# Scaling and shifting the float64 weights' upper words on GpSimd instead of VectorE, in a linear-attention and feed-forward kernel

## The chip, the cores and the metric

The kernel runs on one core of one Trainium2 chip, in one launch. The metric is the device time of one execution in microseconds (us): before the change the median of three runs is 903.01 us (902.7 to 903.02). The engines are called by the names of the profile: PE is TensorE (PEld its weight loads), DVE is VectorE, ACT is ScalarE, POOL is GpSimd, SP is SyncE, which here only starts DMAs.

## The reference

```python
# q, k, v: (8, 8, 576, 64) float32; g_norm: (64,); w_in: (512, 2048), w_out: (2048, 512), both float64
kv  = np.einsum('bhsd,bhse->bhde', k, v)
out = np.einsum('bhsd,bhde->bhse', q, kv)
rms = np.sqrt(np.mean(out * out, axis=-1, keepdims=True) + 1e-06)
x = (out / rms * g_norm).transpose(0, 2, 1, 3).reshape(4608, 512)
h  = x @ w_in
sp = np.maximum(h, 0.0) + np.log1p(np.exp(-np.abs(h)))     # softplus
return ((h * erf(sp)) @ w_out).astype(np.float32)
```

The two weight matrices are float64 in memory. The kernel reads each number as two 32-bit words, an upper and a lower one, and makes float32 of them itself.

## The kernel before, in words

**Tiling.** The 4608 tokens are worked through in nine groups of 512 (T = 0 to 8): the first 512 tokens of each of the eight batches, and a ninth group of the eight remainders of 64. For one group the attention gives x, transposed, as four blocks of 128 features by 512 tokens. The hidden width of 2048 is cut into 16 units of 128 (f = 0 to 15). For unit f, PE multiplies x with a block of w_in (tile `h_ps`, line 1021), ACT copies the result and takes its softplus and erf, DVE multiplies the two (`gates`, line 902, tile `h_sb`), and PE multiplies that with a block of w_out into four accumulators (`o_ps`, `project`, line 655), five units later (`LAG`). From T = 1 on, numbers are split into a rounded upper part and a remainder, so that PE can use its faster float32 form (line 599, tiles `n_ps` and `m_ps`); the split weights are written to device memory once and loaded again for later groups.

**The stage that the change touches** is T = 0, after the start-up, from about 32 to 116 us. There the float64 weights are fetched and converted, in 18 steps listed in `w_order`: four steps of one unit of w_in (512 words per partition), then 14 steps of two units (1024 words per partition), alternately of w_in and w_out. I call them by matrix and first unit: in0, in1, in2, in3, in4, out0, in6, out2, in8, out4, in10, out6, in12, out8, in14, out10, out12, out14. Each step has three parts, each of which goes through the list with an index of its own:

- `load_w` (lines 233 and 238) starts the DMA on SP's queue into `w_raw`. That tile has four buffers.
- `w_split` makes `w_m` from the lower words on ACT (line 260). For the first five steps, which fall in the start-up, it also makes `w_e` on ACT, the upper words times 2**-112 as floats (line 259). `w_e` and `w_m` have two buffers each.
- `w_join` finishes the step on DVE: for the later 13 steps (flag `late_`) it makes that product itself (line 270); it shifts `w_e` left by three bits (line 273), puts the sign bit back from the upper words (line 276), and adds `w_m` (line 281) into `w_in_sb` or `w_out_sb`, from which PE reads.

One call of `weights()` runs `w_split`, then `w_join`, then `load_w`, in this order. In the loop over the units the splits are one step ahead of the joins: a call splits step i+1 and joins step i. The order of each engine's instructions is the order in which the program emits them (`manual_schedule`); each engine works through its own list in that order and waits where an operand is not ready.

**Other DVE work of this stage**, placed between the joins, belongs to the attention of group 1, which runs beside: `keep_tail` (lines 433, 360, 361), `halve` (lines 447, 448, tiles `sq_hi` and `sq_lo`), `norm` (lines 483, 486, 495), and the transposition of q (line 336). `sq_hi` and `sq_lo` are read by the PE products of `mean` (lines 463 and 464), and the transposed q by those of `visit` (line 411).

POOL clears two tiles, builds the identity for the transposes, starts six small DMAs and scales one column (line 221), all in the first 11 us, and has nothing after that.

Of the kernel before, what the change touches and what calls it, by code (L numbers as in the profile page):

```python
# [39 lines left out]
FP32 = mybir.dt.float32  # L40
FP32R = mybir.dt.float32r
I32 = mybir.dt.int32
U32 = mybir.dt.uint32
AF = mybir.ActivationFunctionType
ALU = mybir.AluOpType
# [23 lines left out]
def kernel(  # L69
# [10 lines left out]
    nc = tc.nc  # L80
    P = 128
# [3 lines left out]
    G = J * P  # L85
# [7 lines left out]
    const = ctx.enter_context(tc.tile_pool(name="const", bufs=1))  # L93
# [117 lines left out]
    for p in range(NP):  # L211
        nc.gpsimd.dma_start(
            out=q_last[p % 2 * R : p % 2 * R + R, p // 2],
            in_=q[0, 2 * p : 2 * p + 2, G:S, :].rearrange("h r d -> r h d"),
        )
    for i in range(2):
        nc.gpsimd.dma_start(
            out=g_col[i * D : i * D + D, :], in_=g_norm.rearrange("(d one) -> d one", one=1)
        )
    gm_col = const.tile([P, 1], FP32, name="gm_col")  # L220
    nc.gpsimd.tensor_scalar(out=gm_col, in0=g_col, scalar1=-0.5, scalar2=None, op0=ALU.mult)
    x_last = const.tile([P, KC, G], FP32, name="x_last")
# [20 lines left out]
    def words(which, f):  # L243

        raw = w_raw[which, f]
        hi, lo = (
            raw.bitcast(kind).rearrange("p (n two) -> p n two", two=2)[:, :, half]
            for kind, half in ((FP32, 1), (U32, 0))
        )
        return hi, lo, raw.rearrange("p (n two) -> p n two", two=2)[:, :, 1]  # L250

    def w_split(which, f, k):


        hi, lo, _ = words(which, f)
        e = early.tile([P, G * k], I32, name="w_e", tag="w_e", bufs=2)
        m = early.tile([P, G * k], I32, name="w_m", tag="w_m", bufs=2)
        if not w_late:
            nc.scalar.activation(e.bitcast(FP32), hi, AF.Copy, scale=2.0**-112)
        nc.scalar.activation(m, lo, AF.Copy, scale=2.0**-29)  # L260
        w_cv[which, f] = e, m, bool(w_late)

    def w_join(which, f, k):


        scaled, _, hi = words(which, f)
        e, m, late_ = w_cv.pop((which, f))
        w_raw.pop((which, f))
        if late_:
            nc.vector.tensor_scalar(  # L270
                out=e.bitcast(FP32), in0=scaled, scalar1=2.0**-112, scalar2=None, op0=ALU.mult
            )
        nc.vector.tensor_scalar(
            out=e, in0=e, scalar1=3, scalar2=None, op0=ALU.logical_shift_left
        )
        nc.vector.scalar_tensor_tensor(  # L276
            out=e, in0=hi, scalar=-(1 << 31), in1=e, op0=ALU.bitwise_and, op1=ALU.bitwise_or
        )
        out_ = (w_in_sb if which == "in" else w_out_sb)[f // 2][:, f % 2 : f % 2 + k]
        out_ = out_.rearrange("p t f -> p (t f)")  # L280
        nc.vector.tensor_tensor(out=out_.bitcast(I32), in0=e, in1=m, op=ALU.add)  # L281
# [10 lines left out]
    def w_next(what):  # L292
        i = w_at[what]
        if i < len(w_order):
            w_at[what] = i + 1
            {"load": load_w, "split": w_split, "join": w_join}[what](*w_order[i][1:])
# [809 lines left out]
    def part(h, half):  # L1106
        return h[:, :, half * 2 * P : half * 2 * P + 2 * P]
# [35 lines left out]
    for m in range(first_batch, batches + 1):  # L1143
# [81 lines left out]
        for j in range(J):  # L1225
# [3 lines left out]
            if b2 == NB - 1:  # L1229
                e = es.pop(j)  # L1230
# [14 lines left out]
            for half in due_halves:  # L1245
                nc.vector.tensor_tensor(  # L1246
                    out=part(h, half), in0=part(h, half), in1=part(s, half), op=ALU.mult
# [38 lines left out]
```

## Time and profile before

| what | value |
|---|---|
| median of three runs | 903.01 us |
| span of the profiled execution (first to last instruction) | 901.3 us |
| PE busy | 893.6 us, 99% of the span |
| DVE busy | 766.7 us, 85% |
| ACT busy | 595.1 us, 66% |
| POOL busy | 4.7 us, 1%, 14 instructions |
| granted PE clock, mean | 0.999 of full speed |

The profile is of one execution, and its span leaves out what lies around the first and the last instruction: the median of the runs is 1.7 us longer. A line of a timeline gives the start in us, the length in us, the engine, the source line, the operation, the tile written and the tiles read, the shape, and how many instructions are merged; in brackets behind it stand the idle time before it and what ended that. A line of a group gives the summed busy time in us, the mean of one instruction in ns, and the idle time before them. Steps of PE's 128x512 float32 products appear as two instructions each.

### The profile page before, as it was taken

What the parts mean: (1) busy time and instruction counts of PE and PEld (TensorE: products, weight loads), DVE (VectorE), ACT (ScalarE), POOL (GpSimd) and SP (SyncE); (2) the same over time, 40 slices, a digit from 0 to 9 for tenths busy, and PEclk for the clock granted to TensorE, in tenths of its full rate; (3) what the DMA queues carried; (4) which work ended last, traced back from release to release, by engine and by line L of the source; (5) the groups of instructions that cost most, each with busy time, mean ns of one, the idle gap of its engine ahead of it and who ended that gap; (6) DMA issues with size and microseconds to landing.
All of it is one profiled execution on the core that took longest, in us unless ns stands there. A gap on an engine that the chain in (4) does not pass through costs nothing.

```text
span 901.3 us, 13468 instructions
## 1 busy us (share of the span) xinstructions
PE 893.6 (99%) x4962; PEld 672.4 (75%) x4962; DVE 766.7 (85%) x1105; ACT 595.1 (66%) x789; POOL 4.7 (1%) x14
## 2 busy tenths in 40 slices
PE   8999999999999999999999999999999999999998
PEld 4444456666788888888888888888888888888887
DVE  5899978899799888888888888888888888886667
ACT  5976687777766666666766666666666666665552
POOL 2000000000000000000000000000000000000000
PEclk9999999999999999999999999999999999999999
DMA  9977418899699987988899979988897787778871
GB/s 285 295 224 226 108 73 319 305 341 355 233 384 355 347 301 258 382 308 297 273 361 336 320 248 335 365 300 292 286 341 273 270 304 309 286 282 323 317 263 51
DMA packets 136929, 259.89 MB, mean 288 GB/s; under 512 B 78816, under 2 KB 87264, under 8 KB 136864
## 3 DMA queue, kind: packets, MB, share of 16 engines
q1 hardware_dynamic: 136128, 258.09, 81.3%
q8 instruction: 39, 0.64, 0.3%
q10 hardware_dynamic: 544, 0.82, 0.3%
q14 instruction: 26, 0.21, 0.1%
q0 software_dynamic: 192, 0.13, 0.0%
HBM read 224.40 MB, written 34.60 MB: 287 GB/s over the span
## 4 chain that ended last, share of the span: by engine, by line
PE 96%; DMA 1%; DVE 1%; ACT 1%; issue 0%; SPq 0%; DVEq 0%
PE n_ps L599 50%; PE m_ps L599 25%; PE o_ps L655 9%; PE h_ps L1021 5%; PE at_ps L425 2%; PE at_ps L411 2%; PE n_ps L918 1%; PE at_ps L463 1%; PE at_ps L464 1%; DMA q_sb<-in_q_dram 1%; DMA w_raw<-in_moe_w_out_dram 1%; PE o_ps L918 0%; DVE w_e L276 0%; PE o_ps L722 0%; DVE w_in_sb L281 0%; PE ms_ps L729 0%
## 5 line engine op out<-in xcount | busy, mean ns | idle before, releaser
L599 PE MATMUL n_ps<-w_out_parts,g_forms 128*128 128x512 f32 (+1 forms) x936 | 230.7, 389 | 0.0
L599 PE MATMUL n_ps<-x_forms,w_in_parts 128*128 128x512 f32 x896 | 223.9, 392 | 0.0
L599 PEld LDWEIGHTS n_ps<-w_out_parts,g_forms 128*128 128x128 f32 x936 | 173.7, 188 | 35.3
L599 PEld LDWEIGHTS n_ps<-x_forms,w_in_parts 128*128 128x128 f32 x896 | 166.6, 188 | 35.3
L574 DVE TENSOR_TENSOR h<-m_ps,h 128x512 f32<-128x512 f32 x116 | 78.2, 687 | 60.3 <-PE m_ps L599 58.1
L599 PE MATMUL m_ps<-w_out_parts,g_forms 128*128 128x512 f32 x464 | 124.0, 389 | 0.0
L599 PE MATMUL m_ps<-x_forms,w_in_parts 128*128 128x512 f32 x448 | 119.7, 389 | 0.0
L1192 ACT ACTIVATE h<-n_ps 128x512 f32<-128x512 f32 x112 | 66.2, 594 | 75.1 <-PE n_ps L599 75.0
L1197 ACT ACTIVATE s<-h 128x512 f32<-128x512 f32 x112 | 68.3, 629 | 70.0 <-DVE h L574 70.0
L599 PEld LDWEIGHTS m_ps<-w_out_parts,g_forms 128*128 128x128 f32 x464 | 87.1, 188 | 18.5
L599 PEld LDWEIGHTS m_ps<-x_forms,w_in_parts 128*128 128x128 f32 x448 | 84.1, 188 | 17.5
L574 DVE TENSOR_TENSOR e<-m_ps,e 128x512 f32<-128x512 f32 x116 | 80.2, 692 | 15.2 <-PE m_ps L599 5.3
L655 PE MATMUL o_ps<-w_out_sb,h_sb 128*128 128x512 f32 x192 | 86.8, 595 | 0.0
L540 DVE SCALAR_TENSOR_TENSOR g_forms<-g_forms 128x1024 fp32r<-128x1024 f32 x58 | 71.1, 1225 | 2.0
L537 DVE TENSOR_TENSOR g_forms<-h,g_forms 128x1024 fp32r<-128x1024 f32 x58 | 70.6, 1217 | 1.2 <-ACT g_forms L534 1.1
L534 ACT ACTIVATE g_forms<-h 128x1024 fp32r<-128x1024 f32 x58 | 58.4, 1049 | 15.5 <-PE m_ps L599 11.1
L569 DVE SCALAR_TENSOR_TENSOR e<-n_ps,e 128x512 f32<-128x512 f32 (+1 forms) x89 | 60.4, 678 | 6.9 <-PE n_ps L599 6.9
L1246 DVE TENSOR_TENSOR h<-h,s 128x1024 f32<-128x1024 f32 x56 | 65.9, 1218 | 0.0
L655 PEld LDWEIGHTS o_ps<-w_out_sb,h_sb 128*128 128x128 f32 x192 | 35.5, 190 | 38.3 <-issue 36.9
L1021 PE MATMUL h_ps<-xT,w_in_sb 128*128 128x512 f32 x128 | 57.9, 596 | 1.1 <-DVE w_in_sb L281 1.1
L115 ACT ACT_TABLE_LOAD x43 | 55.2, 1283 | 0.8
L1220 ACT ACTIVATE s<-s 128x1024 f32<-128x1024 f32 x50 | 50.6, 1053 | 0.3
(148 smaller groups left out, 1018.7 us busy)
## 6 DMA issues: line engine op xcount, KB each, us to landing
w_out_parts<-w_out SPq DMA_DIRECT2D x116, 768.0 KB, 6.8
w_in_parts<-w_in SPq DMA_DIRECT2D x112, 768.0 KB, 6.7
w_in<-w_new SPq DMA_DIRECT2D x16, 768.0 KB, 4.9
k_sb<-in_k_dram SPq DMA_DIRECT2D x32, 288.0 KB, 5.9
v_sb<-in_v_dram SPq DMA_DIRECT2D x31, 288.0 KB, 5.8
w_raw<-in_moe_w_in_dram SPq DMA_DIRECT2D x16, 512.0 KB, 5.9
w_raw<-in_moe_w_out_dram SPq DMA_DIRECT2D x8, 1024.0 KB, 5.1
out_dram<-e SPq DMA_DIRECT2D x32, 256.0 KB, 3.8
```

What stands on the lines that cost most here:

```text
L115: nc.scalar.preload_act_table_set("softplus")
L534: nc.scalar.activation(high, x, AF.Copy, scale=1.0 + 2.0**-13)
L537: nc.vector.tensor_tensor(out=low, in0=x, in1=high.bitcast(FP32), op=ALU.subtract)
L540: nc.vector.scalar_tensor_tensor(out=both, in0=low.bitcast(FP32), scalar=SHIFT, in1=high.bitcast(FP32), op0=ALU.mult, op1=ALU.add,)
L569: nc.vector.scalar_tensor_tensor(out=out_, in0=ps, scalar=scale, in1=out_, op0=ALU.mult, op1=ALU.add)
L574: nc.vector.tensor_tensor(out=out_, in0=ps, in1=out_, op=ALU.add)
L599: nc.tensor.matmul(ps[:, cols], lhsT=weights(form, k), rhs=moving(form, k)[:, cols], start=(form == forms[0] and k == 0), stop=(form == fo ...
L655: nc.tensor.matmul(o_ps[j], lhsT=g[:, j * P : j * P + P], rhs=one(w_out_sb, f), start=(f == 0), stop=last,)
L1021: nc.tensor.matmul(plain[i], lhsT=blocks_of(one(w_in_sb, i % FC))[:, c], rhs=xT[T][:, c, :], start=(c == 0), stop=(c == KC - 1),)
L1192: nc.scalar.activation(h[:, i], n_ps, AF.Copy, scale=SHIFT - 1.0)
L1197: nc.scalar.activation(s[:, i], h[:, i], AF.Softplus)
L1246: nc.vector.tensor_tensor(out=part(h, half), in0=part(h, half), in1=part(s, half), op=ALU.mult)
```

## The change

The product with 2**-112 of the later 13 steps moves from DVE, where `w_join` issued it, to POOL, where `w_split` issues it, one call earlier in the program. The shift by three of these steps becomes a 32-bit integer multiplication by eight on POOL, issued in `w_join`; its second operand is a new column tile `eight`, set once by DVE and read as if it were as wide as the step. The first five steps stay as they were.

```diff
@@ -217,6 +217,8 @@
+    eight = const.tile([P, 1], I32, name="eight")
+    nc.vector.memset(eight, 8)
     gm_col = const.tile([P, 1], FP32, name="gm_col")
@@ -257,6 +259,10 @@  (w_split)
         if not w_late:
             nc.scalar.activation(e.bitcast(FP32), hi, AF.Copy, scale=2.0**-112)
+        else:
+            nc.gpsimd.tensor_scalar(
+                out=e.bitcast(FP32), in0=hi, scalar1=2.0**-112, scalar2=None, op0=ALU.mult
+            )
         nc.scalar.activation(m, lo, AF.Copy, scale=2.0**-29)
@@ -267,12 +273,13 @@  (w_join)
         if late_:
+            nc.gpsimd.tensor_tensor(
+                out=e, in0=e, in1=eight.to_broadcast([P, G * k]), op=ALU.mult
+            )
+        else:
             nc.vector.tensor_scalar(
-                out=e.bitcast(FP32), in0=scaled, scalar1=2.0**-112, scalar2=None, op0=ALU.mult
-            )
-        nc.vector.tensor_scalar(
-            out=e, in0=e, scalar1=3, scalar2=None, op0=ALU.logical_shift_left
-        )
+                out=e, in0=e, scalar1=3, scalar2=None, op0=ALU.logical_shift_left
+            )
         nc.vector.scalar_tensor_tensor(
             out=e, in0=hi, scalar=-(1 << 31), in1=e, op0=ALU.bitwise_and, op1=ALU.bitwise_or
         )
```

## The prediction, made before the changed kernel was run

> **What bounds the kernel now.** I read the page's head first, then busy time by stretches, then the waits and the timelines of the stage that is changed. Head (busy us, share, instructions) and three stretches (start:end, length, busy PE, PEld, DVE, ACT, POOL, clock, DMA share, GB/s):
>
> ```profile
> span 901.3 us, 13468 instructions
> PE 893.6 (99%) x4962; PEld 672.4 (75%) x4962; DVE 766.7 (85%) x1105; ACT 595.1 (66%) x789; POOL 4.7 (1%) x14
> ```
> ```profile
> 50.00:60.00 10.00, 9.62 (x25) 4.41 (x24) 9.66 (x13) 6.53 (x8) 0.00 (x0) 1.00 0.88 277
> 80.00:90.00 10.00, 10.00 (x69) 4.72 (x69) 9.53 (x16) 4.17 (x5) 0.00 (x0) 1.00 0.81 252
> 120.00:901.00 781.00, 777.44 (x4322) 617.32 (x4320) 667.49 (x948) 509.88 (x674) 0.00 (x0) 1.00 0.84 300
> ```
>
> PE is the bound everywhere, and after 120 us it is busy for 777.44 of 781 us: time lost earlier is not made good. DVE is nearly full in the changed stage, yet PE hardly waits for it. PE's only wait there is 0.39 us for in6, and the waits of the whole start and stage for `w_in_sb` are 1.1 us:
>
> ```profile
> 51.15 3.70 PE L1021 MATMUL h_ps<-xT,w_in_sb 128*128 128x512 f32 x8 [0.39 <-DVE w_in_sb L281]
> ...
> 114.63 0.68 PE L463 MATMUL at_ps<-sq_hi,mean_w 128*128 128x256 f32 x1
> ```
> ```profile
> PE h_ps L1021 <- DVE w_in_sb L281: 1.1, 2, 0.7
> ```
>
> So relief of DVE is worth at most some 0.4 us. What counts is whether DVE falls behind, since PE has a margin on it. The end of out0 and the joining of out12 in DVE's timeline, with what stands behind it:
>
> ```profile
> 42.41 1.23 DVE L281 CUSTOM_DVE_ANT_0 w_out_sb<-w_e,w_m 128x2048 uint16<-128x2048 uint16 x1
> ...
> 105.02 0.69 DVE L270 TENSOR_SCALAR w_e<-w_raw 128x1024 f32<-128x1024 f32 x1
> 105.74 0.69 DVE L273 TENSOR_SCALAR w_e<-w_e 128x1024 int32<-128x1024 int32 x1
> 106.47 1.23 DVE L276 SCALAR_TENSOR_TENSOR w_e<-w_raw,w_e 128x1024 int32<-128x1024 int32 x1
> 107.83 1.23 DVE L281 CUSTOM_DVE_ANT_0 w_out_sb<-w_e,w_m 128x2048 uint16<-128x2048 uint16 x1
> 108.97 0.68 DVE L902 TENSOR_TENSOR h_sb<-h_sb,s_sb 128x512 f32<-128x512 f32 x1
> 109.57 0.42 DVE L447 CAST sq_hi<-qT 128x512 fp32r<-128x512 f32 x1
> 110.03 0.69 DVE L448 TENSOR_TENSOR sq_lo<-qT,sq_hi 128x512 fp32r<-128x512 f32 x1
> ```
>
> From the end of out0 (42.41 + 1.23 = 43.64) to that of out12 (107.83 + 1.23 = 109.06) lie 11 steps in 65.42 us, 5.95 us each. `sq_lo` behind out12 ends at 110.72, and PE reads it after 114.63: a margin of 3.9 us. The gate at 104.42 (ends 105.1, wanted by line 655 at 108.06) has 3.0 us, others 3 to 7. The weights have far more from out2 on (out8: 15 us).
>
> **What leaves DVE.** 13 pairs of lines 270 and 273 at 0.72 us each from start to start (105.02, 105.74, 106.47): 13 x 1.45 = 18.8 us. PE waits for none of it but in6, so its worth is 0 to 0.4 us.
>
> **What comes to POOL.** It shows no such instruction, so I bound both by its small ones (mean ns of one before the bar's idle time):
>
> ```profile
> L210 POOL MEMSET bd_kv<- 128x256 f32 x1 | 0.3, 311 | 0.0
> masks.py:199 POOL TENSOR_SCALAR_AFFINE_SELECT ident<-ident 128x128 f32<-128x128 f32 x1 | 0.3, 292 | 0.1
> L221 POOL TENSOR_SCALAR gm_col<-g_col 128x1 f32<-128x1 f32 x1 | 0.2, 218 | 4.9 <-DMA g_col<-in_g_norm_dram 4.9
> masks.py:197 POOL MEMSET ident<- 128x128 f32 x1 | 0.2, 205 | 0.3 <-POOLq L1267 0.3
> ```
>
> The memsets give (311 - 205) / 128 = 0.83 ns a word and 99 ns fixed. One input, 128 words, takes 292 ns. If 218 ns of that is fixed (line 221), a word costs 0.58 ns and the scaling of 1024 words 0.81 us; if only 99 ns is, 1.51 ns and 1.64 us. I take the middle, 1.2 us. The multiplication reads two tensors: at least 0.8 us, as if the second were free; at most twice 1.51 ns a word, 3.2 us; I take two readings, 2 x 1.2 - 0.2 = 2.2 us. The pair is 3.4 us (1.6 to 4.8).
>
> **The new wait.** In POOL's list the scaling of step i+1 stands ahead of the multiplication of step i. The scaling needs the `w_e` buffer that line 281 of step i-1 frees, and line 276 of step i now waits for the multiplication. So the steps form a ring: line 281, POOL's pair, line 276, line 281. Its DVE part is 109.06 - 106.47 = 2.59 us; three handovers at 0.05 (PE started at 51.15 after DVE's end at 51.10) make some 0.2. One turn is 2.59 + 3.4 + 0.2 = 6.19 us, and 11 turns 68.1 against 65.4: DVE is 2.7 us late at out12. Behind the waiting line 276 on DVE are queued line 281, the gates, and group 1's `halve` and `norm`; PE waits for gates and `sq_lo`. The first turn costs nothing: in6's DMAs are issued by 31.7 us and take 5.9 (median), POOL would be through with scaling in6 and multiplying out0 at 37.6 + 3.4 = 41.0, and line 276 ran at 41.05.
>
> **Other DVE work during POOL's pair.** If DVE and POOL can read memory at once, that work lies beside the pair. If not, it lengthens the ring. DVE's instructions with two tensors from SBUF, or at double rate, between the ends of out0 and out12 are nine gates at 0.60 (108.97 to 109.57), three of line 486 at 0.72, and two of `halve` at 1.07 (109.57 to 110.64): 5.4 + 2.2 + 2.1 = 9.7 us. No row shows the engines together: the bounds are 0 and 9.7. The nearest rows are lines 273 and 276: one tensor of 1024 words takes 0.69 us, two take 1.23, so DVE alone has no third stream to spare. I take 9.7 and keep 0 for the range.
>
> [...]
>
> **Edits at nothing.** Setting `eight` is 0.06 us (line 203's length, the same shape) in DVE's 3.8 us of idle time before 6.22. SP's load for step i+4 is issued when line 276 of step i ends, with group 1's q, k and v behind it; four steps are some 24 us and a landing 5 to 8, so a slip of a few us stays hidden; uncovered, it would hold PE at line 411 by its own length. ACT's line 260 waits for `w_m` in the same ring, and copies of `h_ps` stand behind it; ACT idles 1.5, 5.3 and 6.5 us before the copies at 84, 93 and 115, and `h_ps` has two buffers. The new tile may shift others in SBUF; no row prices that, I take 0.
>
> **Sum.** 2.7 + 9.7 = 12.4 us late at out12, less the margin of 3.9: PE loses 8.5 us, in pieces from about 85 us on. The profiled execution becomes 901.3 + 8.5 = 909.8 and the median, 1.7 above its span as before, 911.5. This case alone spans 905 to 919.
>
> **Rivals.**
> *The pair fits (not slower).* Without blocking, 2.7 us late is under 3.9 and PE never waits: 903.0, or 902.6 if in6's wait also goes. It decides as long as blocking plus 11 x (pair - 3.16) stays below 3.9 us. For it: DVE's order leaves 3.4 us beside the weights in each step. Against it: half of that work has two inputs.
> *POOL is slow.* At 4.8 us a pair the ring is 7.59, 11 turns 83.5, 18.1 late; with blocking and the margin 18.1 + 9.7 - 3.9 = 23.9: 927. The point is a pair above 4 us. For it: an integer product of full words, of which POOL shows no row.
> *The relief counts.* If DVE's 18.8 us were on the path it would be faster; PE's busy rows from 60 to 110 us, full in every stretch, speak against it.
>
> **How the numbers follow.** Forecast 0.50, slow POOL 0.22, the pair fits 0.24, faster by something unseen 0.04. About 0.2% (1.8 us) is what a measurement can tell from no change; the fitting pair lies within it, so slower has 0.72. The range goes from 902.4 (the pair fits) to 926, leaving out the end of slow POOL and a real gain, some 0.15.
>
> **What would show it.** Right: POOL's pairs stand back to back in every step, lines 276 wait for POOL, steps are over 6.2 us apart, gates lie late or long, PE waits for `sq_lo` and gates between 85 and 116 us, and DVE's busy time falls by about 18 us. Wrong: a pair below 3 us, gates and POOL overlapping at their old lengths, or PE's loss after 120 us.

## The result, and the profile after

The changed kernel takes 932.71 us (median of four runs, 931.31 to 934.05) against 903.01 us: a ratio of 1.033, with a 95% interval of 1.0317 to 1.0343. The forecast was 911.5 us, range 902.4 to 926. The direction was right, the size was not: 29.7 us were lost where 8.5 were expected, and the time lies beyond the range.

In the changed file the lines behind the new code are seven higher: the scaling is line 263, the multiplication 276, the sign line 283, the addition 288, the gates 909, PE's unit products 1028, the projection 662, the mean 470. The head of the page after, and the busy time by stretches (start:end, length, busy PE, PEld, DVE, ACT, POOL, clock, DMA share, GB/s):

```profile
span 930.6 us, 13490 instructions
PE 907.6 (98%) x4962; PEld 675.9 (73%) x4962; DVE 756.6 (81%) x1080; ACT 595.7 (64%) x789; POOL 69.6 (7%) x40
```
```profile
50.00:60.00 10.00, 7.47 (x20) 3.49 (x19) 3.29 (x4) 6.02 (x8) 7.12 (x4) 1.00 0.55 171
90.00:100.00 10.00, 7.03 (x55) 3.36 (x50) 4.53 (x5) 2.72 (x4) 5.65 (x3) 0.83 0.45 121
150.00:930.00 780.00, 776.35 (x4309) 615.13 (x4307) 663.05 (x943) 505.10 (x668) 0.00 (x0) 1.00 0.87 298
```

PE is no longer full in the stage, and POOL is busy in 7 of 10 us there. DVE is idle for more than half of a stretch in which it was 97% busy. In the second stretch even the granted clock is below 1 (0.83). The waits of the start and the stage (who waited for whom: us in all, times, longest) say for what:

```profile
DVE w_e L283 <- POOL w_e L276: 35.2, 10, 4.7
PE o_ps L662 <- DVE h_sb L909: 6.5, 4, 3.0
PE at_ps L470 <- DVE bd_kv L368: 4.9, 2, 2.9
PE h_ps L1028 <- DVE w_in_sb L288: 3.5, 3, 2.5
```

That is the ring of the prediction: PE for DVE, DVE for POOL. One turn of it on POOL, without and with a gate beside it, then the last ones on DVE and the last wait of PE:

```profile
62.44 2.88 POOL L263 TENSOR_SCALAR w_e<-w_raw 128x1024 f32<-128x1024 f32 x1 [2.71 <-DVE w_out_sb L288]
65.26 1.92 POOL L276 TENSOR_TENSOR w_e<-w_e,eight 128x1024 int32<-128x1024 int32 x1
70.32 3.26 POOL L263 TENSOR_SCALAR w_e<-w_raw 128x1024 f32<-128x1024 f32 x1 [3.13 <-DVE w_in_sb L288]
73.55 1.88 POOL L276 TENSOR_TENSOR w_e<-w_e,eight 128x1024 int32<-128x1024 int32 x1
```
```profile
44.25 1.23 DVE L283 SCALAR_TENSOR_TENSOR w_e<-w_raw,w_e 128x1024 int32<-128x1024 int32 x1 [4.05 <-POOL w_e L276]
45.62 1.22 DVE L288 CUSTOM_DVE_ANT_0 w_out_sb<-w_e,w_m 128x2048 uint16<-128x2048 uint16 x1
...
132.19 1.23 DVE L288 CUSTOM_DVE_ANT_0 w_out_sb<-w_e,w_m 128x2048 uint16<-128x2048 uint16 x1
...
135.85 0.29 DVE L368 TENSOR_TENSOR bd_kv<-at_ps,kv_other 128x128 f32<-128x128 f32 x1
```
```profile
136.29 0.55 PE L470 MATMUL at_ps<-sq_hi,mean_w 128*128 128x256 f32 x1 [2.85 <-DVE bd_kv L368]
...
137.28 6.17 PE L662 MATMUL o_ps<-w_out_sb,h_sb 128*128 128x512 f32 x8
```

The scaling takes 2.85 to 2.88 us where no gate runs beside its start and 3.2 to 3.3 where one does (as in the last two lines on POOL); the multiplication takes 1.9. out0's joining now ends at 46.84 and out12's at 133.42: 11 turns in 86.58 us, 7.87 each, where there were 65.42 us.

The 29.3 us by which the span grew come apart at two marks of PE. The last wait ends at 136.29, where the same product began at 114.63 before: 21.7 us, start-up included. From there to the first product of T = 1 2.7 us more are lost, nearly all in the eight projections at 137.28, which took 3.59 us before and 6.17 now. That product before and after:

```profile
128.82 0.80 PE L599 MATMUL n_ps<-x_high,w_new 128*128 128x512 f32 x1
```
```profile
153.19 0.79 PE L606 MATMUL n_ps<-x_high,w_new 128*128 128x512 f32 x1
```

From that product to the end lie 772.5 us before and 777.4 after: 4.9 us, all of them without a wait.

### The profile page after: what moved, and what is told of

Same layout as the page of the kernel before. It is cut to its first block, busy times and chain, and to the rows that moved or that the text cites. A ratio compares the mean times of both kernels' runs of the same rounds, so it can differ in the third digit from the quotient of the medians.

```text
span 930.6 us, 13490 instructions
## 1 busy us (share of the span) xinstructions
PE 907.6 (98%) x4962; PEld 675.9 (73%) x4962; DVE 756.6 (81%) x1080; ACT 595.7 (64%) x789; POOL 69.6 (7%) x40
## 4 chain that ended last, share of the span: by engine, by line
PE 87%; POOL 6%; issue 3%; DVE 1%; ACT 1%; DMA 1%; SPq 0%; POOLq 0%; DVEq 0%
PE n_ps L606 49%; PE m_ps L606 24%; PE o_ps L662 6%; POOL w_e L263 4%; POOL w_e L276 2%; PE h_ps L1028 2%; PE at_ps L432 2%; PE at_ps L418 2%; PE n_ps L925 1%; PE at_ps L470 1%; DMA q_sb<-in_q_dram 1%; PE at_ps L471 1%; DVE w_e L283 1%; PE o_ps L925 0%; DVE w_out_sb L288 0%
## 5 line engine op out<-in xcount | busy, mean ns | idle before, releaser
L606 PE MATMUL n_ps<-w_out_parts,g_forms 128*128 128x512 f32 (+1 forms) x936 | 230.9, 389 | 0.0
L606 PE MATMUL n_ps<-x_forms,w_in_parts 128*128 128x512 f32 x896 | 226.6, 395 | 0.0
L662 PE MATMUL o_ps<-w_out_sb,h_sb 128*128 128x512 f32 x192 | 94.2, 638 | 6.5 <-DVE h_sb L909 6.5
L662 PEld LDWEIGHTS o_ps<-w_out_sb,h_sb 128*128 128x128 f32 x192 | 38.2, 205 | 50.1 <-issue 41.1
L283 DVE SCALAR_TENSOR_TENSOR w_e<-w_raw,w_e 128x1024 int32<-128x1024 int32 (+1 forms) x18 | 22.5, 1247 | 36.9 <-POOL w_e L276 35.2
```

The costliest lines, as they stand in the source:

```text
L606: nc.tensor.matmul(ps[:, cols], lhsT=weights(form, k), rhs=moving(form, k)[:, cols], start=(form == forms[0] and k == 0), stop=(form == fo ...
L662: nc.tensor.matmul(o_ps[j], lhsT=g[:, j * P : j * P + P], rhs=one(w_out_sb, f), start=(f == 0), stop=last,)
```

## The experiments

Each kernel is compared with the kernel before on the same chip; its median was 903.0 to 903.2 us.

**The new tile's place.** The loss behind the stage had no wait in it, and the loads had become slower; so I looked at the one thing that stays after the stage, the tile `eight` ahead of others in memory. To the kernel before I added only:

```diff
+    eight = const.tile([P, 1], I32, name="eight")
+    nc.vector.memset(eight, 8)
     gm_col = const.tile([P, 1], FP32, name="gm_col")
```

> The kernel before with the column tile eight and its memset added, and nothing on POOL. In the changed kernel the products of T = 1 to 8 take 4.5 us longer without any wait (PE busy 773.15 us from the first product of T = 1 on, against 768.64 before), loads into SBUF land later (w_in_parts 7.7 us against 6.7), and the start-up is 0.5 us longer. Theory place: this comes from where the new tile pushes the tiles behind it, so this kernel takes 903.0 + 5 = 908 us with landings of 7.7 us. Rival: it comes from the later timing of the stage or from the chip's state, and this kernel takes 903.0 within 0.5 us, landings 6.7 us.

It took 907.95 us, ratio 1.0051 (1.0038 to 1.0065). A line of a DMA group gives KB each and us from issue to landing; first the lines of the kernel before:

```profile
w_out_parts<-w_out SPq DMA_DIRECT2D x116, 768.0 KB, 6.8
w_in_parts<-w_in SPq DMA_DIRECT2D x112, 768.0 KB, 6.7
```
```profile
L599 PE MATMUL n_ps<-x_forms,w_in_parts 128*128 128x512 f32 x896 | 223.9, 392 | 0.0
L599 PE MATMUL m_ps<-x_forms,w_in_parts 128*128 128x512 f32 x448 | 119.7, 389 | 0.0
```

With the new tile:

```profile
PE 898.8 (99%) x4962; PEld 673.2 (74%) x4962; DVE 766.6 (85%) x1106; ACT 595.5 (66%) x789; POOL 4.7 (1%) x14
```
```profile
w_out_parts<-w_out SPq DMA_DIRECT2D x116, 768.0 KB, 7.7
w_in_parts<-w_in SPq DMA_DIRECT2D x112, 768.0 KB, 7.8
```
```profile
L601 PE MATMUL n_ps<-x_forms,w_in_parts 128*128 128x512 f32 x896 | 226.6, 395 | 0.0
L601 PE MATMUL m_ps<-x_forms,w_in_parts 128*128 128x512 f32 x448 | 121.2, 392 | 0.0
```

PE is busy 5.2 us longer with the same products. It is mainly the products with w_in's parts that grew (223.9 and 119.7 us before; 4.2 of the 5.2 us), not those with w_out's, whose buffers are laid out from the other end of the memory and did not move (230.9 after 230.7). The loads of w_out's parts landed later all the same, so a later landing alone did not lengthen the products. So a tile of one column cost 4.9 us, and none of it is POOL's.

The other way round, the changed kernel without the unused tile `pad` ahead of `eight`:

```diff
-    const.tile([P, 8], FP32, name="pad")
```

> The changed kernel without the unused tile pad, which stands ahead of eight in the same pool, so that the tiles behind lie where they lay before. Theory place: 932.7 - 5 = 927.7 us, landings of w_in_parts back to 6.7 us, PE busy after the first product of T = 1 back to 768.6 us; the rest of the loss, some 24.7 us, stays. Rival (the tile's place does nothing): 932.7 us.

It took 922.99 us, ratio 1.0229 (1.0203 to 1.0255): 9.7 us less than the changed kernel, though its four runs spread from 921.43 to 928.05. Landings of `w_in_parts` are back at 6.6 us. The gain is larger than the place alone: with the loads earlier, POOL scales in6 at 36.46 rather than 39.51, line 282 for out0 runs at 41.20 rather than 44.25, and only two stretches of half clock are left.

How far may the tiles move? An unused tile of 64, 512 or 2048 bytes a partition in the kernel before, and `eight` with 32 bytes more ahead of w_in's buffers:

```diff
+    const.tile([P, 16], I32, name="eight")     # 512 bytes: [P, 128]; 2048 bytes: [P, 512]
     gm_col = const.tile([P, 1], FP32, name="gm_col")
```

> The kernel before with an unused tile of 64 bytes a partition where the changed kernel has eight (which takes 32 with its rounding, as pad does). Theory line: what costs 4.9 us is that the tiles behind start 32 bytes off a multiple of 64; a shift by 64 costs nothing: 903.1 us, landings 6.7 us. Rival (any shift from the old places costs): 906 to 908 us.

> The kernel before with an unused tile of 512 bytes a partition at the place of eight. Shifts of 32 and 64 bytes cost 4.9 and 4.1 us. If what counts is a start at a multiple of 512 bytes or less, this takes 903 us and w_in_parts land in 6.7 us; if the multiple is larger, or the old places matter for another reason, 906 to 908 us with landings of 7.4 us or more.

> The same with 2048 bytes, the length of one buffer row of 512 words. If what counts is where the tiles start within 2048 bytes, this takes 903 us with landings of 6.7 us; if any move from the old places costs, 906 to 908 us.

64 bytes cost as much as 32, nearly: 907.04 us (ratio 1.0045, 1.003 to 1.006), landings 7.4 us; a shift by 64 is no protection, and that theory fell. 512 bytes cost nothing: 903.06 us (0.9999, 0.999 to 1.0008), landings 6.8; nor do 2048: 902.8 us (1.0, 0.999 to 1.0009). And `eight` with the 32 bytes more:

```diff
+    eight = const.tile([P, 1], I32, name="eight")
+    nc.vector.memset(eight, 8)
...
+    ctx.enter_context(tc.tile_pool(name="shift_w", bufs=1)).tile([P, 8], FP32, name="shift_w")
     w_in_p = ctx.enter_context(tc.tile_pool(name="w_in_p", bufs=BATCH))
```

> The kernel before with eight (908.0 us by the earlier run) and a further 32 bytes ahead of the buffers of the loaded weights of w_in (and what lies behind them), so that these start at multiples of 64 again while the tiles for k, v, q, x and the sums do not. If the weights' loads are what makes PE's products slower, landings go back to 6.7 us and the time to 903.5 to 904.5 us (0.5 us is the start-up's). If it is x and the others, it stays near 908.

This missed both expectations: 910.9 us (1.0088, 1.0073 to 1.0103), landings 8.0, w_in's products 229.1 and 122.7 us. It moves w_in's buffers by 64 bytes in all and x's by 32, and is worse than moving both by 32 or both by 64. Which of the two tiles of a product counts stays open.

Landings took 7.4 to 8.0 us after shifts of 32 and 64 bytes, 6.8 and 6.9 after 512 and 2048. No shift between 64 and 512 bytes was run, so where the loss ends is not shown. Nor is it shown why the loads landed later: those of w_out's parts, which were not moved, did so as well (7.6 to 7.8 us against 6.8). Why PE's products slow down too, no run shows.

**The ring.** First the order of POOL's two instructions, the multiplication of step i ahead of the scaling of step i+1:

```diff
...
         else:
+            times_eight()                      # the multiplication for the step before
             nc.gpsimd.tensor_scalar(
                 out=e.bitcast(FP32), in0=hi, scalar1=2.0**-112, scalar2=None, op0=ALU.mult
             )
+            to_eight.append((e, k))
...
         if late_:
-            nc.gpsimd.tensor_tensor(
-                out=e, in0=e, in1=eight.to_broadcast([P, G * k]), op=ALU.mult
-            )
+            if to_eight and to_eight[0][0] is e:
+                times_eight()
```

> The changed kernel with POOL's two instructions the other way round: the multiplication of step i is issued ahead of the scaling of step i+1, so a joining no longer waits for the next step's scaling. Theory ring: the loss of the stage comes from both instructions (3.2 + 1.9 us) lying between the end of one joining and the start of the next; now two steps share a ring of 2.6 + 5.1 + 0.3 = 8 us, far under 2 x 5.95, PE never waits, and the time is that of place alone, 908 us. Theory lock: DVE's two-input instructions and POOL's cannot run at once; a step needs 2.46 (lines 283 and 288) + 0.9 (gates, halve, norm) + 5.1 (POOL) = 8.5 us whatever the order, so 2.5 us x 11 - 3.9 = 23 us are lost besides place, 931 us.

911.23 us, ratio 1.0089 (1.0075 to 1.0102): of the 29.7 us, 21.5 are gone by order alone, with the same instructions. That is near theory ring's 908 and far from theory lock's 931; the 3.3 us over 908 are waits of PE (3.1 us in three places). Yet the engines do hinder each other. On DVE and on POOL in this kernel:

```profile
67.28 2.81 DVE L293 SCALAR_TENSOR_TENSOR w_e<-w_raw,w_e 128x1024 int32<-128x1024 int32 x1
```
```profile
67.11 1.89 POOL L259 TENSOR_TENSOR w_e<-w_e,eight 128x1024 int32<-128x1024 int32 x1
```

The sign line, 1.23 us alone, began 0.17 us behind a multiplication and ended at 70.09, 1.09 us after POOL's end at 69.00: it stood until POOL was through. DVE's busy time is 772.7 us here, 16 more than in the changed kernel, and it has room for that.

Then a third buffer of `w_e`, POOL's order unchanged:

```diff
-        e = early.tile([P, G * k], I32, name="w_e", tag="w_e", bufs=2)
+        e = early.tile([P, G * k], I32, name="w_e", tag="w_e", bufs=3)
...
```

> The changed kernel with three buffers of w_e in place of two, POOL's order as changed: the scaling of step i+1 no longer waits for the end of joining i-1 but for that of i-2, so POOL can run ahead. Theory ring: POOL needs 5.1 us a step, under 5.95, DVE does not wait, 908 us (place alone). Theory lock: as with the other order, some 931 us. If three buffers help and the other order does not, or the reverse, the two ways into the ring are not equal and the waits of line 283 tell which is left.

918.18 us, ratio 1.0168 (1.0151 to 1.0185), between the two. The turns no longer wait for the buffer, but the first one still has the scaling of in6 ahead of the multiplication of out0, and in6's load was not there until 41.03:

```profile
DVE w_e L283 <- POOL w_e L276: 6.0, 1, 6.0
```

One wait of 6.0 us is all that is left, and PE waits 7.0 us for gates. So the ring has two ways in, the buffer and POOL's order; the order cures both.

**The parts alone**, tiles placed as before. Only the scaling on POOL:

```diff
-        if late_:
-            nc.gpsimd.tensor_tensor(
-                out=e, in0=e, in1=eight.to_broadcast([P, G * k]), op=ALU.mult
-            )
-        else:
-            nc.vector.tensor_scalar(
-                out=e, in0=e, scalar1=3, scalar2=None, op0=ALU.logical_shift_left
-            )
+        nc.vector.tensor_scalar(
+            out=e, in0=e, scalar1=3, scalar2=None, op0=ALU.logical_shift_left
+        )
```

> Tiles placed as before (no pad). Only the scaling is on POOL, still issued one step ahead; the shift by three is again DVE's, in the joining. Theory ring: without the multiplication nothing of joining i stands behind the scaling of step i+1 on POOL; the scaling has a whole step more, DVE does not wait, and the time is that of before, 903 us within 1. Rival (a slow POOL instruction by itself, 3.2 us a step beside DVE's two-input work, delays DVE by sharing memory): above 906 us, with lines 282 and 287 or the gates much longer than 1.23 and 0.68 us.

902.17 us (ten runs), ratio 0.999 (0.998 to 0.9999). The slower of the two instructions costs nothing, since nobody waits for it: with a step of lead, 3.1 us on POOL lie beside DVE's work. Nor does it relieve DVE by much: 13 instructions of 0.68 us left DVE, yet its busy time fell only from 766.7 to 766.0 us, since others took longer beside POOL:

```profile
68.52 3.30 POOL L262 TENSOR_SCALAR w_e<-w_raw 128x1024 f32<-128x1024 f32 x1 [3.54 <-DVE w_out_sb L282]
```
```profile
68.95 1.69 DVE L274 TENSOR_SCALAR w_e<-w_e 128x1024 int32<-128x1024 int32 x1
70.67 1.23 DVE L277 SCALAR_TENSOR_TENSOR w_e<-w_raw,w_e 128x1024 int32<-128x1024 int32 x1
```

The shift at the scaling's start took 1.69 us in place of 0.69; the sign line behind it had its usual length. The kernel takes away in6's wait (PE has no listed wait in the stage) and is the fastest kernel of this study, 1 us below the kernel before, at the edge of what the runs can tell.

Only the multiplication on POOL, the scaling on DVE right ahead of it:

```diff
-        else:
-            nc.gpsimd.tensor_scalar(
-                out=e.bitcast(FP32), in0=hi, scalar1=2.0**-112, scalar2=None, op0=ALU.mult
-            )
...
         if late_:
+            nc.vector.tensor_scalar(
+                out=e.bitcast(FP32), in0=scaled, scalar1=2.0**-112, scalar2=None, op0=ALU.mult
+            )
             nc.gpsimd.tensor_tensor(
```

> Tiles placed as before (no pad). Only the multiplication is on POOL; the scaling is again DVE's, in the joining, right ahead of it. Theory ring: DVE waits for the whole multiplication in each step, since nothing stands between its scaling and the sign line: 1.9 us and two handovers more, 0.72 less, so 5.95 becomes 7.3 us; 11 steps are 15 us late, less 3.9 of margin: 11 us of waits of PE, and 1.7 us for each 3.4 us at half clock: 914 to 918 us. Rival (only the scaling is too slow): 903 to 906 us.

915.0 us, ratio 1.0131 (1.0117 to 1.0145), as expected. DVE stands still for the whole of it, once in each of 13 steps:

```profile
DVE w_e L281 <- POOL w_e L274: 26.1, 13, 2.0
```

Both cures, the other order and the tiles' old place:

```diff
-    const.tile([P, 8], FP32, name="pad")
...
         else:
+            times_eight()                      # the rest as in the order's own diff above
```

> Both cures at once: the multiplication of step i ahead of the scaling of step i+1 on POOL, and the tile pad taken out so that the tiles behind eight lie as before. The other order alone took 911.2 us, the tile's place alone costs 908.0 - 903.1 = 4.9 us. Theory (the two causes add): 911.2 - 4.9 = 906.3 us or less, with PE waits of at most 3 us in the stage and full clock throughout. Rival (the two are not independent, as the changed kernel without pad, which gained 9.7 us, hints): 903 to 904 us, since earlier landings also take away the remaining waits.

905.95 us, ratio 1.003 (1.0019 to 1.0042): with the ring gone the two causes add (911.2 - 4.9 = 906.3); with it, the place alone was worth 9.7. Moving both instructions still costs 2.8 us, with 2.3 us of waits of PE.

**Why the scaling is slow.** Reading 1024 adjacent words (of x, so the weights are not scaled and the result is another one) in place of every second one, without `pad`:

```diff
-                out=e.bitcast(FP32), in0=hi, scalar1=2.0**-112, scalar2=None, op0=ALU.mult
+                out=e.bitcast(FP32).rearrange("p (t f) -> p t f", t=2),
+                in0=xT[0][:, 0:2, :],
+                scalar1=2.0**-112,
+                scalar2=None,
+                op0=ALU.mult,
```

> The changed kernel without pad, but POOL's scaling reads 1024 adjacent words of the tile xT in place of every second word of w_raw, so the weights are wrong and the first scalings wait for no load; it shows what the step between the words costs. If the step of two words makes the scaling slow, it falls from 2.85 us (no DVE work beside) to 1.2 to 1.6 us, the pair from 5.1 to some 3.4, the turn from 7.8 to 6.2, and the time to 903 to 907 us. If the scaling is slow in itself, it stays at 2.8 us or more and the time at 923 us.

921.37 us, ratio 1.0202 (1.0188 to 1.0216), against 922.99 for the changed kernel without `pad`, and the scaling takes 2.77 us without a gate beside it: the distance of two words is worth 0.08 us. Then the product of the weights again, without `pad`, as one of two tensors, the constant in a second column of `eight` read as wide as the step:

```diff
...
-            nc.gpsimd.tensor_scalar(
-                out=e.bitcast(FP32), in0=hi, scalar1=2.0**-112, scalar2=None, op0=ALU.mult
-            )
+            nc.gpsimd.tensor_tensor(
+                out=e.bitcast(FP32), in0=hi, in1=small.to_broadcast([P, G * k]), op=ALU.mult
+            )
```

> Tiles placed as before (no pad). The changed kernel with the scaling issued as a two-tensor product, the second operand a column of 2**-112 read as wide as the step, like the multiplication by eight. If the form of the instruction (tensor with a constant) is what makes the scaling slow, it takes 1.9 us like the multiplication, the pair 3.8 in place of 5.1, a turn 6.5 in place of 7.8 us: 11 x 0.55 = 6 us late, less 3.9 of margin, 905 to 908 us. If floats are what makes it slow, it stays at 2.8 us or more and the time at 923 us.

```profile
57.94 1.91 POOL L264 TENSOR_TENSOR w_e<-w_raw,eight 128x1024 f32<-128x1024 f32 x1 [2.70 <-DVE w_out_sb L289]
```

1.91 us, floats and all: it is the form with a constant that is slow, 2.85 us. The time fell to 916.7 (ratio 1.0163, 1.0146 to 1.018), not to the 905 to 908 that I expected. The turns are 7.3 us long (11 in 80.50 us, from 44.28 to 124.78), not 6.5, because beside the two-tensor products DVE waited more:

```profile
65.70 2.13 DVE L455 CAST sq_hi<-qT 128x512 fp32r<-128x512 f32 x1
67.86 2.26 DVE L456 TENSOR_TENSOR sq_lo<-qT,sq_hi 128x512 fp32r<-128x512 f32 x1
```

These two take 0.42 and 0.69 us in the kernel before; here they ended at 67.83 and 70.12, each just behind one of POOL's products (67.54 and 69.58). What the shorter scaling gained, some 0.9 us a turn, was partly given back in this way.

**The clock.** In the changed kernel PE ran at half clock in four stretches behind its waits, three of 3.4 us and one of 6.8. I filled the waits with dummy products:

```diff
+    def fill_next(n, times):
+        plain[n + 1] = ps_h.tile([P, G], FP32, name="h_ps", tag="h")
+        for _ in range(times):
+            nc.tensor.matmul(plain[n + 1], lhsT=blocks_of(one(w_in_sb, 0))[:, 0],
+                             rhs=xT[0][:, 0, :], start=True, stop=True)
...
```

> The changed kernel (932.7 us) with ten dummy products of 0.86 us on PE (8.6 us in all) where PE waits for DVE: three ahead of unit 10's projection, two in unit 11, two ahead of unit 13's projection, three in unit 14, written to the bank that the next unit starts anew. The changed kernel's clock was at half in four stretches right behind these waits, 17.1 us together, worth 8.5 us. Theory clock: a PE that is not idle keeps its clock; the half-clock stretches go and the time falls by 5 to 8.5 us, to 924 to 928, although PE has 8.6 us more to do. Rival (the products after the waits are slow for another reason): no half-clock stretch goes and the time is 932.7 us or more.

931.67 us (931.23 to 934.51), no faster by what the runs can tell. The clock did what theory clock says: in the windows of the first three stretches it is 0.50 in the changed kernel and 1.00 here. The first and the third of them, in the changed kernel, then in this one, with the last stretch at half clock that is left there:

```profile
94.70:98.00 3.30, 3.30 (x5) 1.33 (x4) 0.00 (x0) 1.24 (x3) 3.30 (x2) 0.50 0.79 245
125.40:128.70 3.30, 3.30 (x5) 1.35 (x4) 0.00 (x0) 1.30 (x3) 3.30 (x2) 0.50 0.00 0
```
```profile
94.70:98.00 3.30, 3.30 (x9) 1.52 (x8) 0.00 (x0) 1.64 (x4) 3.30 (x2) 1.00 0.90 294
125.40:128.70 3.30, 3.30 (x9) 1.39 (x9) 0.00 (x0) 1.81 (x4) 3.30 (x2) 1.00 0.00 0
137.60:140.80 3.20, 3.20 (x5) 1.22 (x4) 2.99 (x5) 1.66 (x3) 0.00 (x0) 0.50 0.00 0
```

But the time did not follow, and my 5 to 8.5 us were wrong: the ring paces PE, so a slower PE only shortens its next wait. DVE's line 368 ends at 136.65 here and at 136.14 in the changed kernel. Only the stretch behind the last wait costs, 2.7 us in the changed kernel; of that, one stretch of 3.4 us in place of 6.8 remains here, and a new one came at 55.7 us behind a wait that I had not filled.

## Why the prediction was wrong, point by point

**Right.** PE hardly waited for DVE before, and relief of DVE was worth little: 0.4 us at most by the forecast, and the kernel with the scaling alone gained 1.0, with an interval from 0.1 to 1.8. The loss comes from a ring of line 288, POOL's pair and line 283, and 11 turns of it against a fixed margin. PE waits for gates and at the mean. DVE's busy time fell, by 10 us (forecast 18; the rest is in instructions lengthened beside POOL).

**Wrong, and the largest: the price of the scaling.** I took 1.2 us, with bounds of 0.81 and 1.64, from an instruction of another form over 128 words. It is 2.85 us, beyond the upper bound. The multiplication, taken at 2.2, is 1.9. The pair is 4.75 in place of 3.4: 11 x 1.35 = 14.8 us. The rival of a slow POOL had a pair of 4.8 and 927 us, so its mechanism and its pair were near, but for the wrong half of the pair: I blamed the integer product. That its time was near as well is partly luck: it had 9.7 us for the blocking, far too much, and nothing for the first turn, the tile's place and the clock.

**The blocking.** I added 9.7 us, an estimate: the gates, line 486 and `halve` counted whole, as if none of them could run beside POOL's pair. No run shows that. In the changed kernel the turns took 86.58 us, and 11 x (2.59 + 4.75 + 0.2) would be 82.9: 3.6 us. Nearly half of that is the last turn, where out12's sign line took 2.90 us in place of 1.23 beside out14's multiplication; the rest is covered by POOL's own scaling, which took some 0.4 us longer in the eight turns where a gate ran beside its start. While the scaling ran, DVE's two-tensor instructions were not held until its end (line 493 at 62.98 took 1.15 us for its usual 0.69 and ended at 64.13, the scaling at 65.32); beside two-tensor products they could be, and there (the scaling as a tensor product) 11 x (2.59 + 3.8 + 0.2) = 72.5 against 80.5 leaves 8 us. So the term depends on the form on POOL's side, of which the prediction said nothing.

**The first turn.** I put it at nothing, since 37.6 + 3.4 = 41.0 met line 276's 41.05. POOL began to scale in6 at 39.51 in place of 37.6, since the loads were later by the tile's place (without `pad` it began at 36.46), and the pair took 4.75, so it came to 44.25: 3.2 us.

**The margin.** 3.9 us was that of `sq_lo`. PE waited for line 368, four instructions later on DVE, which reads the tile that the mean's product then writes. In the kernel before, this line ended at 111.78, a margin of 2.85:

```profile
111.49 0.29 DVE L361 TENSOR_TENSOR bd_kv<-at_ps,kv_other 128x128 f32<-128x128 f32 x1
```

**The tile's place.** I took 0 and said that no row prices it. It cost 4.9 us in the kernel that has only the new tile, more than any other term that I had at nothing.

**The clock.** Not in the sum: 2.7 us behind the last wait.

Together: turns 21.2 late, first turn 3.2, less the margin of 2.85, is 21.5 at the last wait (21.7 measured); 2.7 and 4.9 more make 29.3, the growth of the span.

## What to carry to other kernels

An instruction moved to an idle engine is paid by its place in the chains, not by its length: the 2.85 us scaling cost nothing with a step of lead, and the 1.9 us multiplication cost 12 us where DVE waited for it; so issue what is awaited ahead of what prepares the next step. Price a form of instruction by a row of that very form, or leave the range open upwards. Don't count the relief of the engine that the work leaves before you have looked at what runs beside it. And see whether a new tile, however small, moves others in memory: here it cost nothing when it took its bytes from an unused one. Look at the landings of loads after any change.

## What the runs showed of the hardware that I had not expected

- On POOL a product of 1024 words a partition with a constant took 2.85 to 2.88 us where no gate ran beside its start, and one of two tensors, the second a column read over and over, 1.9 us in the changed kernel. Adjacent words made the first 2.77.
- Beside a two-tensor product on POOL, DVE's sign line, its cast and the line of `sq_lo` stood until POOL ended (2.81 us for 1.23, 2.13 for 0.42, 2.26 for 0.69). Not every two-tensor line did: line 500, which reads `at_ps`, took its usual 0.68 us at 75.36 in the kernel with the other order, while POOL multiplied from 74.82 to 77.20. Beside the scaling with a constant none of the three stood until its end: what began near its start took up to 1 us longer, and what began later took its usual time. In the changed kernel, while POOL scaled from 70.32 to 73.58, the cast took 1.38 us, and the two-tensor line 455 its usual 0.69.

```profile
70.75 1.38 DVE L454 CAST sq_hi<-qT 128x512 fp32r<-128x512 f32 x1
72.16 0.69 DVE L455 TENSOR_TENSOR sq_lo<-qT,sq_hi 128x512 fp32r<-128x512 f32 x1
```

- In the changed kernel waits of PE of 2.1 to 3.0 us were followed by 3.4 or 6.8 us at half clock, one of 2.5 us at 52 us was not; in the kernel with dummy products one of 1.98 us before 136.79 was, and one of 2.14 us before 105.23 was not. So no length of wait divides them here. The slower products cost time only where no wait followed: 2.7 us behind the last one.
- Tiles moved by 32 or 64 bytes made loads land 10 to 19% later (7.4 to 8.0 us for 6.7) and PE's products with them 1 to 2.5% longer (226.6 and 229.1 us for 223.9); after shifts of 512 or 2048 bytes landings stayed within 3%, and the kernels took 903.06 and 902.8 us, as before.
